# One more unit of the first MLP layer by seven products in four stages, and a pair of transposes moved

## The chip, the cores and the metric

The kernel runs on one core of a Trainium2 chip. The metric is the device time of one execution in microseconds (us), lower is better. The core has TensorE (PE, with its weight loads shown as PEld), VectorE (DVE), ScalarE (ACT), GpSimd (POOL) and SyncE (SP); each works through a queue of its own in order, and DMA transfers are issued from the queues of SP and POOL (and, at the very end, ACT).

## The reference

Attention with a forget gate, followed by a two-layer MLP with tanh-GELU. In the kernel the products are in bf16 with sums in f32.

```python
# q, k, v: (8, 8, 576, 64); f: (8, 8, 576)
scores = q @ k.T / sqrt(64)
cum = cumsum(log(clip(f, 1e-4, 1)))
attn = softmax(where(causal, scores + cum[:, None] - cum[None, :], -1e9))
x = (attn @ v).transpose(0, 2, 1, 3).reshape(4608, 512)
h = x @ w_in                      # 512 x 2048
out = gelu_tanh(h) @ w_out        # 2048 x 512, out is (4608, 512) f32
```

## The kernel before

The attention is done for 16 groups i of four heads (two groups in each of the 8 batches), the MLP for 9 chunks c of 512 rows. A batch has 576 rows and a chunk 512, so the attention runs somewhat ahead. Nothing is scheduled by a planner: a table of words, one for each stage, is the program order, and every engine takes its own instructions from it in that order (`play`). The front table does groups 0 to 6 and chunks 0 and 1; then stage c, for c from 2 to 8, plays `TABLES[c]`: the rest of the second layer of chunk c-1, the first layer of chunk c, and the second layer of chunk c mixed with the attention of groups q2 = 2c+2, q3 = 2c+3 and q4 = 2c+4. Stages 2 to 6 have attention work, 7 and 8 none.

The words that matter here:

- `P.k`: one pair of the first layer, 256 of the 2048 columns of h for the 512 rows: 8 products on PE of 512 columns each (two blocks of 128 columns of h, four input blocks), into a two-bank PSUM tile of pool psS (`P.k.1`: the tile of pool psO, which the attention's outputs use too), then one GELU on ACT (L369, L376).
- `R.k`: a unit by seven products, three words long. It gives the same as the pairs P.k and P.(k+4) in Strassen's manner (Winograd's form): seven blocks of four products with 256 columns (`multiply`, L417) into four half tiles pa, pb (pool psS) and pc, pd (pool psM), with five passes on DVE between them (L432, L423) and four GELUs (L428). The order of the blocks is pa, pb, pc, pd, pa in the first word, pc in the second, pd in the third.
- `T`: four subtractions of blocks of x for the unit of the next chunk, on DVE, 128 x 512 elements each (`x_sums`, L390). They are written over the x of the chunk that is done.
- `K.k.n`: one of the four sums of blocks of w_in that unit k needs (`w_sums`, L405), on DVE. Sums 0 to 2 are written over the x of an old chunk (`HOMES`), sum 3 over a block of w_in itself, after which the plain pairs P.k and P.(k+4) can't be done any more.
- `O`, `F`, `f`: so many steps of the second layer, also by seven products (`seven_products`, L504). O.512 is what is left of the last chunk; its last step ends with an addition on DVE (L529) that frees a bank of pool psM, and a store.
- `G`: sums of the GELU outputs on DVE (L483 to L489). `X` and `Y`: ACT's tables for exp and GELU.
- `S.i.r`: scores of a third of a group on PE and exp on ACT (L256, L264). `M.i.r`: causal masks on POOL (L270). `D`, `V`: denominators and outputs, products on PE, then DVE (L343 to L347, L355). `VW.i`: the values weighted, on POOL (L210). `CL.i`: a copy of a part of them on DVE (L215).
- `TK.i`, `TQ.i`: transposes of k and q on DVE (L193). `LK.i`, `LQ.i`: loads of them, issued by POOL (L187), into buffers that the transposes of two groups before have read. `LV`: loads of v, issued by SP (L164).

Both pools of PSUM that the unit uses have two tiles: psS with tag s (scores, pairs, pa and pb) and psM with tag m (second layer, pc and pd).

Of the kernel before, what the change touches and what calls it, by code (L numbers as in the profile page):

```python
# [16 lines left out]
def kernel(  # L17
# [53 lines left out]
    """  # L71

    FRONT = """
        TQ.0 B.2.256 TK.1 SB TR LP.2@LQ.0 B.2.128 CW S.0.0 B.5.384 B.1.256 Z TQ.1 vw.0.0 S.0.2 WI.0 LQ.2 M.0.0 B.3.384 H.1.0.1
        LP.3 B.1.256 vw.1.0 WI.1@LU.4 W H.1.1.1 WI.3 B.2.256 WI.2 H.1.0.0 M.1.0.1 D.0.0 M.1.0.0 H.0.1.1 V.0.0.0 H.0.1.0 B.2.256 M.0.1 H.1.1.0 V.0.1.0
        D.1.0 H.0.3.0 B.2.128 V.1.0.0 LX.1.1 H.0.3.1 V.1.1.0 m.0.3.2 H.1.3.0 m.0.3.4 B.1.256 VW.1.1 H.1.3.1 B.4.128 vw.0.1 D.0.1 M.1.3 S.1.2 M.1.1 LK.2
        V.0.1.1 V.0.0.1 WO.0 J.0.1 D.1.1 J.0.0 WO.1@LV.1.1 V.1.1.1 V.1.0.1 J.0.3 WO.2@WI.1 VW.3 J.1.0 WO.3 LK.3 LQ.3 J.1.1 TQ.2 J.1.3 LQ.4
        LX.1.0@WO.2 TK.2 J.0.2 J.1.2 X LK.4 F.0.6 TK.3 B.3.256 S.2.0 LK.5 F.0.9 S.2.2 F.0.10 S.2.1 TQ.3 TQ.4 F.0.10 LV.2.0@LK.5 m.2.1 vw.2
        TK.4 S.3.0 f.0.1 M.2.2 CL.2 LQ.5 M.2.0 D.2 f.0.6 S.3.1 m.3.0 F.0.6 V.2.0 S.3.2 TK.5 LK.6 M.3.2 f.0.7 V.2.1 CL.3
        S.4.1 m.3.1 LQ.6 F.0.6 TQ.5 H.4.2.1 D.3 H.4.0.1 LQ.7 VW.4 H.4.0.0 V.3.1 v.3.0 f.0.3 H.4.2.0 CL.4 I.1.0 m.4.1 U.0 LV.2.1@LQ.5 I.1.4  # L80
        TQ.6 m.4.2.3 I.1.1 I.1.5 U.1 LV.3.0@LQ.7 m.4.2.2 TK.6 G.0 M.4.0 I.1.2 I.1.3 U.3 I.1.6 I.1.7 G.1.1.2 U.2 X F.1.14 S.5.0 f.1.28 S.5.1 D.4 M.5.0 f.1.16
# [2 lines left out]
    """

    HOMES = {1: 0, 3: 1}
    TABLES = {}
    TABLES.update(dict.fromkeys((2, 5), """
        Y O.512 P.0 P.1 TK.q3 TQ.q3 LK.q5 LQ.q5 TK.q4 TQ.q4 LK.q6 LQ.q6 LV P.4 P.5 G.0 P.2 P.3 P.6 P.7 G.1.1.2 X F.10 S.q3.0
        D.q2 M.q3.0 f.22 S.q3.1 V.q2.0 M.q3.1 VW.q3 f.18 S.q3.2 V.q2.1 M.q3.2 CL.q3 f.16 S.q4.0 D.q3 M.q4.0 f.18 S.q4.1 V.q3.0  # L90
        M.q4.1 VW.q4 f.9 V.q3.1 f.7 S.q4.2 M.q4.2 CL.q4
    """))
    TABLES.update(dict.fromkeys((3,), """
        Y O.512 P.0 P.1 TK.q3 TQ.q3 LK.q5 LQ.q5 TK.q4 TQ.q4 LK.q6 LQ.q6 LV K.1.0 K.1.1 K.1.2 P.4 P.5 G.0 P.2 P.3 P.6 P.7 G.1.1.2
        X F.10 S.q3.0 D.q2 M.q3.0 f.22 S.q3.1 V.q2.0 M.q3.1 VW.q3 f.18 S.q3.2 V.q2.1 M.q3.2 CL.q3 f.16 S.q4.0 D.q3 M.q4.0 f.18
        S.q4.1 V.q3.0 M.q4.1 VW.q4 f.9 V.q3.1 f.7 S.q4.2 M.q4.2 CL.q4
    """))
    TABLES.update(dict.fromkeys((4,), """
        Y O.512 P.0 P.1 TK.q3 TQ.q3 LK.q5 LQ.q5 TK.q4 TQ.q4 LK.q6 LQ.q6 LV K.3.0 K.3.1 K.3.2 P.4 P.5 G.0 P.2 P.3 P.6 P.7 G.1.1.2
        X F.10 S.q3.0 D.q2 M.q3.0 f.22 S.q3.1 V.q2.0 M.q3.1 VW.q3 f.18 S.q3.2 V.q2.1 M.q3.2 CL.q3 f.16 S.q4.0 D.q3 M.q4.0 f.18  # L100
        S.q4.1 V.q3.0 M.q4.1 VW.q4 f.9 V.q3.1 f.7 S.q4.2 M.q4.2 CL.q4
    """))
    TABLES.update(dict.fromkeys((6,), """
        Y O.512 P.0 P.1 TK.q3 TQ.q3 LK.q5 LQ.q5 LV P.4 P.5 G.0 P.2 P.3 P.6 P.7 G.1.1.2 X F.10 S.q3.0 D.q2 M.q3.0 f.22 S.q3.1
        V.q2.0 M.q3.1 VW.q3 f.18 S.q3.2 V.q2.1 M.q3.2 CL.q3 f.16 D.q3 f.18 V.q3.0 v.q3.1 T K.1.3 K.3.3 f.18
    """))
    TABLES.update(dict.fromkeys((7,), """
        Y O.512 P.0.1 R.1 P.4.1 R.1 R.1 R.3 P.2.1 R.3 G.0.1.2 P.6 R.3 G.0.3.4 G.1.1.2 T
    """))
    TABLES.update(dict.fromkeys((8,), """  # L110
        O.512 P.0.1 R.1 P.4.1 R.1 R.1 R.3 P.2.1 R.3 G.0.1.2 P.6 R.3 G.0.3.4 G.1.1.2
    """))

    singles = ctx.enter_context(tc.tile_pool(name="singles", bufs=1))
    ostage_pool = ctx.enter_context(tc.tile_pool(name="ostage", bufs=3))
# [664 lines left out]
```

## Time and profile before

| | before |
|---|---|
| time, median of 3 runs | 330.25 us (330.21 to 332.17) |
| profiled execution, its span | 328.4 us |
| PE busy | 316.9 us (96%), 5421 products |
| DVE busy | 206.4 us (63%), 323 instructions |
| ACT busy | 201.7 us (61%) |
| POOL busy | 110.6 us (34%) |
| stages 2 to 6 by the starts of their first layers | 34.85, 34.48, 34.48, 34.48, 32.86 us |
| stages 7 and 8 | 25.74 us, 29.09 us to the end |
| first layer of a stage with eight pairs | 13.81 us |
| first layer of stages 7 and 8 (four pairs, two units) | 13.03 and 13.01 us |
| granted TensorE clock | 1.00 throughout |

The profile shows one execution; its span lies 1.85 us below the median of the timed runs. Busy time of PE counts the pipelined products with modelled ends; the steps from start to start in the chain of waits tell the time that a product takes of the stream. Stage starts (first product of P.0) are at 102.42, 137.27, 171.75, 206.23, 240.71, 273.57 and 299.31 us. A group in the timeline names line, engine, operation, output and inputs, shapes and count.

### The profile page before, as it was taken

The page shows a single profiled execution, that of the slowest core. Times are in us where ns is not written, and L with a number is a line of the kernel's source. Part 1 is how long each engine was busy: PE and PEld are TensorE (multiplying, and loading weights), DVE is VectorE, ACT ScalarE, POOL GpSimd, SP SyncE. Part 2 cuts the span into 40 slices and gives each one's busy share as a digit, 9 for nine tenths or more (in the row PEclk, how much of TensorE's full clock was granted, in tenths as well). Part 3 has the DMA queues.
Part 4 walks back from the last instruction along what each step waited for, and adds up shares of the span by engine and source line. Part 5 has one row for each costly group of instructions (what it writes and reads, how often), then busy time and mean ns, then how long its engine had stood idle before and what let it go on. Part 6 is the DMA issues. An engine that isn't in the chain of part 4 may idle for free.

```text
span 328.4 us, 11961 instructions
## 1 busy us (share of the span) xinstructions
PE 316.9 (96%) x5421; PEld 206.5 (63%) x5421; DVE 206.4 (63%) x323; ACT 201.7 (61%) x231; POOL 110.6 (34%) x155
## 2 busy tenths in 40 slices
...
GB/s 123 210 214 215 168 230 199 167 165 24 36 40 94 236 208 31 94 187 108 37 68 182 140 37 36 160 122 36 36 66 0 36 21 81 2 32 98 0 35 96
DMA packets 44323, 33.42 MB, mean 102 GB/s; under 512 B 27488, under 2 KB 37856, under 8 KB 44272
## 3 DMA queue, kind: packets, MB, share of 16 engines
...
q8 instruction: 42, 0.69, 0.9%
...
## 4 chain that ended last, share of the span: by engine, by line
PE 86%; DMA 3%; DVE 3%; ACT 3%; POOL 2%; issue 2%; POOLq 0%; DVEq 0%; ACTq 0%
PE ps_h L369 29%; PE ps_w L504 25%; PE po L324 9%; PE ps_s L256 8%; PE pso L574 4%; PE ps_h L458 4%; DMA v_nat<-in_v_dram 2%; PE ps_cd L417 2%; ACT pt L264 2%; PE ps_ab L417 2%; PE po_m L310 1%; POOL vw L210 1%; DMA out_dram<-o_st 1%; POOL v_nat L164 0%; PE ps_o L324 0%
## 5 line engine op out<-in xcount | busy, mean ns | idle before, releaser
L264 ACT ACTIVATE pt<-ps_s 128x1024 bf16<-128x1024 f32 (+2 forms) x100 | 93.7, 988 | 39.4 <-PE ps_s L256 34.9
L369 PE MATMUL ps_h<-xT,w_in_sb 128*128 128x512 bf16 x448 | 99.0, 379 | 0.0
L376 ACT ACTIVATE gT<-ps_h 128x1024 bf16<-128x1024 f32 x56 | 57.2, 1022 | 49.9 <-PE ps_h L369 48.3
L270 POOL TENSOR_SCALAR_AFFINE_SELECT pt<-pt 128x512 bf16<-128x512 bf16 (+3 forms) x65 | 38.2, 597 | 132.9 <-ACT pt L264 131.8
L369 PEld LDWEIGHTS <-w_in_sb 128*128 128x128 bf16 x448 | 43.8, 98 | 50.1 <-issue 0.4
L504 PEld LDWEIGHTS <-gT 128*32 128x32 bf16 (+1 forms) x1253 | 50.9, 97 | 6.4 <-issue 1.7
L504 PE MATMUL ps_w<-w_out_sb,gT 128*32 128x256 bf16 (+1 forms) x1056 | 46.9, 273 | 0.0
L504 PEld LDWEIGHTS <-gsum 128*32 128x32 bf16 (+1 forms) x1256 | 38.9, 97 | 2.7 <-issue 1.4
L256 PE MATMUL ps_s<-qT,kT 32*128 32x64 bf16 (+5 forms) x896 | 36.8, 263 | 0.3 <-ACT pt L264 0.2
L483 DVE TENSOR_TENSOR gsum<-gT 128x1024 bf16<-128x1024 bf16 x16 | 11.0, 689 | 35.2 <-ACT gT L376 35.2
L504 PE MATMUL ps_w<-usum,gsum 128*32 128x256 bf16 (+1 forms) x832 | 30.7, 273 | 1.0 <-ACT snap L525 0.7
L355 DVE TENSOR_TENSOR xT<-po,rb 128x576 bf16<-128x576 f32 x26 | 19.6, 755 | 18.9 <-PE po L324 18.6
L193 DVE STREAM_TRANSPOSE kT<-k_c 128x576 f32<-128x576 f32 x16 | 20.0, 1247 | 17.8 <-DMA k_c<-in_k_dram 17.8
L210 POOL TENSOR_TENSOR vw<-v_nat,wT 128x1280 bf16<-128x1280 f32 (+1 forms) x13 | 30.4, 2338 | 0.1
L529 DVE TENSOR_TENSOR o_st<-ps_w,snap 128x512 f32<-128x512 f32 x31 | 21.3, 689 | 13.2 <-PE ps_w L504 11.8
L256 PEld LDWEIGHTS <-kT 32*128 32x128 bf16 x896 | 16.9, 93 | 17.4 <-issue 12.6
L324 PE MATMUL po<-pt,vw 128*32 128x64 bf16 (+4 forms) x624 | 22.5, 279 | 0.0
L324 PEld LDWEIGHTS <-vw 128*32 128x32 bf16 x672 | 14.3, 96 | 10.6 <-issue 3.7
L193 DVE STREAM_TRANSPOSE qT<-q_c 128x576 f32<-128x576 f32 x16 | 19.9, 1242 | 1.1 <-PE ps_s L256 0.5
L164 POOL DMA_DIRECT2D v_nat<-in_v_dram x20 | 15.3, 776 | 4.6 <-DMA w_out_sb<-in_moe_w_out_dram 4.6
L504 PE MATMUL ps_w<-usum,gT 128*128 128x256 bf16 (+1 forms) x197 | 16.4, 273 | 0.0
L574 PE MATMUL pso<-w_out_sb,gT 128*32 128x512 bf16 (+1 forms) x115 | 15.6, 380 | 0.0
...
## 6 DMA issues: line engine op xcount, KB each, us to landing
...
```

The source lines that it names most:

```text
L193: nc.vector.transpose(out=dst.rearrange("p s c -> p (s c)").bitcast(FP32) .rearrange("p (t a) -> p a t", a=S // 32), in_=src.rearrange("p ...
L210: eng.tensor_mul(vw[i % 2][:, t0:t1], vb[:, t0:t1, h0:h0 + 4, :], wT[:, i, t0:t1, :].unsqueeze(3).to_broadcast([128, t1 - t0, 4, D]))
L256: nc.tensor.matmul(tiles[h // 2][:, h % 2, c0:c0 + nq], key_columns(i, key, h, c), qq[32 * h:32 * h + 32, q0:q0 + nq, c], start=(c == 0 an ...
L264: nc.scalar.activation(p[:, 2 * g:2 * g + 2, off:off + n], t[:, :, 0:n], AF.Exp, scale=scale)
L270: nc.gpsimd.affine_select(out=x, in_=x, compare_op=ALU.is_ge, fill=0.0, base=0, pattern=pattern, channel_multiplier=-1)
L324: nc.tensor.matmul(po[r0:r0 + w.shape[-1], 448 + q0:448 + q0 + nq], w, p[:, h, col:col + nq], start=(key in (0, "low")), stop=(key in ("lo ...
L355: nc.vector.tensor_mul(xT[:, 2 * u + x, S * b + s0:S * b + s1], po, rbs[i, part])
L369: nc.tensor.matmul(ph[:, j, :], w_in_sb[:, dt, 128 * ft:128 * ft + 128], xT[:, dt, CH * c:CH * (c + 1)], start=(dt == 0), stop=(dt == N_DT ...
L376: nc.scalar.activation(gT[:, 2 * pr:2 * pr + 2, :], ph, AF.Gelu_apprx_tanh)
L504: nc.tensor.matmul(ps[c0:c0 + width, n, cols[0]:cols[1]], x[:, j, 128 * n + c0:128 * n + c0 + width], w[:, j, cols[0]:cols[1]], start=(fir ...
L529: nc.vector.tensor_add(st, ps, kept[name])
L574: nc.tensor.matmul(pso[c0:c0 + cols, :], gT[:, ft, 128 * n + c0:128 * n + c0 + cols], w_out_sb[:, ft, :], start=(ft == 0), stop=(ft == N_F ...
```

## The change

Unit 1 is done by seven products in stages 3 to 6 too, where before it was done so only in stages 7 and 8; so P.1 and P.5 go there, P.0 and P.4 use the tile of pool psO, and T stands at the end of stages 2 to 5 (at the end of stage 6 it stood before). The weight sums of unit 1 (K.1), which stood in the first layer of stage 3 and at the end of stage 6, move into stage 2. Those of unit 3 (K.3.0 to K.3.2) move from the first layer of stage 4 to places behind V steps of the same stage. In stages 3 to 5 TK.q4 and TQ.q4 move from before the rest of the first layer to behind V.q2.0, and LK.q6 and LQ.q6 to behind M.q3.2; TK.q3, TQ.q3, LK.q5, LQ.q5 and LV now follow the unit. The front table has the same words in other line breaks. Line numbers below L112 grow by 4.

The tables of stage 2 to 6, before and after (the parts that stay the same within a table are left out):

```diff
 # stage 2
-  ... S.q3.1 V.q2.0 M.q3.1 VW.q3 f.18 S.q3.2 V.q2.1 M.q3.2 CL.q3 ... S.q4.1 V.q3.0
-  M.q4.1 VW.q4 f.9 V.q3.1 f.7 S.q4.2 M.q4.2 CL.q4
+  ... S.q3.1 V.q2.0 K.1.0 M.q3.1 VW.q3 f.18 S.q3.2 V.q2.1 K.1.1 M.q3.2 CL.q3 ... S.q4.1 V.q3.0 K.1.2
+  M.q4.1 VW.q4 f.9 V.q3.1 f.7 S.q4.2 M.q4.2 CL.q4 K.1.3 T
 # stages 3 and 5 (K.1.0 K.1.1 K.1.2 in stage 3 alone)
-  Y O.512 P.0 P.1 TK.q3 TQ.q3 LK.q5 LQ.q5 TK.q4 TQ.q4 LK.q6 LQ.q6 LV K.1.0 K.1.1 K.1.2 P.4 P.5 G.0 P.2 P.3 P.6 P.7 G.1.1.2
-  X F.10 S.q3.0 D.q2 M.q3.0 f.22 S.q3.1 V.q2.0 M.q3.1 VW.q3 f.18 S.q3.2 V.q2.1 M.q3.2 CL.q3 f.16 S.q4.0 D.q3 M.q4.0 f.18
-  S.q4.1 V.q3.0 M.q4.1 VW.q4 f.9 V.q3.1 f.7 S.q4.2 M.q4.2 CL.q4
+  Y O.512 P.0.1 R.1 P.4.1 R.1 R.1 TK.q3 TQ.q3 LK.q5 LQ.q5 LV P.2 G.0 P.3 P.6 P.7 G.1.1.2 X F.10 S.q3.0 D.q2 M.q3.0 f.22 S.q3.1 V.q2.0 TK.q4 TQ.q4
+  M.q3.1 VW.q3 f.18 S.q3.2 V.q2.1 M.q3.2 LK.q6 LQ.q6 CL.q3 f.16 S.q4.0 D.q3 M.q4.0 f.18 S.q4.1 V.q3.0 M.q4.1 VW.q4 f.9 V.q3.1 f.7 S.q4.2 M.q4.2
+  CL.q4 T
 # stage 4: as stages 3 and 5, and
-  ... LV K.3.0 K.3.1 K.3.2 P.4 P.5 ...
+  ... V.q2.1 K.3.0 M.q3.2 ... V.q3.0 K.3.1 M.q4.1 VW.q4 f.9 V.q3.1 K.3.2 f.7 S.q4.2 M.q4.2 CL.q4 T
 # stage 6
-  Y O.512 P.0 P.1 TK.q3 TQ.q3 LK.q5 LQ.q5 LV P.4 P.5 G.0 P.2 P.3 P.6 P.7 G.1.1.2 X F.10 ...
-  ... f.16 D.q3 f.18 V.q3.0 v.q3.1 T K.1.3 K.3.3 f.18
+  Y O.512 P.0.1 R.1 P.4.1 R.1 R.1 TK.q3 TQ.q3 LK.q5 LQ.q5 LV P.2 G.0 P.3 P.6 P.7 G.1.1.2 X F.10 ...
+  ... f.16 D.q3 f.18 V.q3.0 v.q3.1 T K.3.3 f.18
```

Stages 7 and 8 keep their tables (two units each, 1 and 3). Over the whole program PE gets 4 x 28 products of 256 columns for 4 x 16 of 512, DVE 4 x 9 more passes (five in a unit, four in T), and ACT four GELUs of half size for two in each of the four stages.

More of the change, by code (lines that the diff above doesn't have):

```diff
@@ L73 @@
     FRONT = """
[L74 to L81, printed above, removed]
@@ L82 @@
-        S.5.2 V.4.0 m.5.2.3 f.1.10 VW.5 V.4.1 CL.5 m.5.2.2 LQ.8 S.6.0 f.1.10 M.5.1 D.5 f.1.7 S.6.1 V.5.1 f.1.12 V.5.0 vw.6 S.6.2
-        m.6.1 M.6.2.2 m.6.0 m.6.2.3 LK.7 LK.8 CL.6 LX.3.1@LK.6
+        TQ.0 B.2.256 TK.1 SB TR LP.2@LQ.0 B.2.128 CW S.0.0 B.5.384 B.1.256 Z TQ.1 vw.0.0 S.0.2 WI.0 LQ.2 M.0.0 B.3.384 H.1.0.1 LP.3 B.1.256 vw.1.0
+        WI.1@LU.4 W H.1.1.1 WI.3 B.2.256 WI.2 H.1.0.0 M.1.0.1 D.0.0 M.1.0.0 H.0.1.1 V.0.0.0 H.0.1.0 B.2.256 M.0.1 H.1.1.0 V.0.1.0 D.1.0 H.0.3.0 B.2.128
+        V.1.0.0 LX.1.1 H.0.3.1 V.1.1.0 m.0.3.2 H.1.3.0 m.0.3.4 B.1.256 VW.1.1 H.1.3.1 B.4.128 vw.0.1 D.0.1 M.1.3 S.1.2 M.1.1 LK.2 V.0.1.1 V.0.0.1 WO.0
@@ new lines @@
+        J.0.1 D.1.1 J.0.0 WO.1@LV.1.1 V.1.1.1 V.1.0.1 J.0.3 WO.2@WI.1 VW.3 J.1.0 WO.3 LK.3 LQ.3 J.1.1 TQ.2 J.1.3 LQ.4 LX.1.0@WO.2 TK.2 J.0.2 J.1.2 X
+        LK.4 F.0.6 TK.3 B.3.256 S.2.0 LK.5 F.0.9 S.2.2 F.0.10 S.2.1 TQ.3 TQ.4 F.0.10 LV.2.0@LK.5 m.2.1 vw.2 TK.4 S.3.0 f.0.1 M.2.2 CL.2 LQ.5 M.2.0 D.2
+        f.0.6 S.3.1 m.3.0 F.0.6 V.2.0 S.3.2 TK.5 LK.6 M.3.2 f.0.7 V.2.1 CL.3 S.4.1 m.3.1 LQ.6 F.0.6 TQ.5 H.4.2.1 D.3 H.4.0.1 LQ.7 VW.4 H.4.0.0 V.3.1
+        v.3.0 f.0.3 H.4.2.0 CL.4 I.1.0 m.4.1 U.0 LV.2.1@LQ.5 I.1.4 TQ.6 m.4.2.3 I.1.1 I.1.5 U.1 LV.3.0@LQ.7 m.4.2.2 TK.6 G.0 M.4.0 I.1.2 I.1.3 U.3
@@ L84 @@
+        I.1.6 I.1.7 G.1.1.2 U.2 X F.1.14 S.5.0 f.1.28 S.5.1 D.4 M.5.0 f.1.16 S.5.2 V.4.0 m.5.2.3 f.1.10 VW.5 V.4.1 CL.5 m.5.2.2 LQ.8 S.6.0 f.1.10 M.5.1
+        D.5 f.1.7 S.6.1 V.5.1 f.1.12 V.5.0 vw.6 S.6.2 m.6.1 M.6.2.2 m.6.0 m.6.2.3 LK.7 LK.8 CL.6 LX.3.1@LK.6
     """
@@ L87 @@
     TABLES = {}
-    TABLES.update(dict.fromkeys((2, 5), """
-        Y O.512 P.0 P.1 TK.q3 TQ.q3 LK.q5 LQ.q5 TK.q4 TQ.q4 LK.q6 LQ.q6 LV P.4 P.5 G.0 P.2 P.3 P.6 P.7 G.1.1.2 X F.10 S.q3.0
-        D.q2 M.q3.0 f.22 S.q3.1 V.q2.0 M.q3.1 VW.q3 f.18 S.q3.2 V.q2.1 M.q3.2 CL.q3 f.16 S.q4.0 D.q3 M.q4.0 f.18 S.q4.1 V.q3.0
-        M.q4.1 VW.q4 f.9 V.q3.1 f.7 S.q4.2 M.q4.2 CL.q4
-    """))
-    TABLES.update(dict.fromkeys((3,), """
-        Y O.512 P.0 P.1 TK.q3 TQ.q3 LK.q5 LQ.q5 TK.q4 TQ.q4 LK.q6 LQ.q6 LV K.1.0 K.1.1 K.1.2 P.4 P.5 G.0 P.2 P.3 P.6 P.7 G.1.1.2
-        X F.10 S.q3.0 D.q2 M.q3.0 f.22 S.q3.1 V.q2.0 M.q3.1 VW.q3 f.18 S.q3.2 V.q2.1 M.q3.2 CL.q3 f.16 S.q4.0 D.q3 M.q4.0 f.18
-        S.q4.1 V.q3.0 M.q4.1 VW.q4 f.9 V.q3.1 f.7 S.q4.2 M.q4.2 CL.q4
@@ L97 @@
[L97 to L105, printed above, removed]
@@ L106 @@
-    """))
-    TABLES.update(dict.fromkeys((7,), """
+    TABLES[2] = """
+        Y O.512 P.0 P.1 TK.q3 TQ.q3 LK.q5 LQ.q5 TK.q4 TQ.q4 LK.q6 LQ.q6 LV P.4 P.5 G.0 P.2 P.3 P.6 P.7 G.1.1.2 X F.10 S.q3.0 D.q2 M.q3.0 f.22 S.q3.1
+        V.q2.0 K.1.0 M.q3.1 VW.q3 f.18 S.q3.2 V.q2.1 K.1.1 M.q3.2 CL.q3 f.16 S.q4.0 D.q3 M.q4.0 f.18 S.q4.1 V.q3.0 K.1.2 M.q4.1 VW.q4 f.9 V.q3.1 f.7
+        S.q4.2 M.q4.2 CL.q4 K.1.3 T
+    """
+    TABLES[3] = """
+        Y O.512 P.0.1 R.1 P.4.1 R.1 R.1 TK.q3 TQ.q3 LK.q5 LQ.q5 LV P.2 G.0 P.3 P.6 P.7 G.1.1.2 X F.10 S.q3.0 D.q2 M.q3.0 f.22 S.q3.1 V.q2.0 TK.q4 TQ.q4
+        M.q3.1 VW.q3 f.18 S.q3.2 V.q2.1 M.q3.2 LK.q6 LQ.q6 CL.q3 f.16 S.q4.0 D.q3 M.q4.0 f.18 S.q4.1 V.q3.0 M.q4.1 VW.q4 f.9 V.q3.1 f.7 S.q4.2 M.q4.2
+        CL.q4 T
@@ new lines @@
+    """
+    TABLES[4] = """
+        Y O.512 P.0.1 R.1 P.4.1 R.1 R.1 TK.q3 TQ.q3 LK.q5 LQ.q5 LV P.2 G.0 P.3 P.6 P.7 G.1.1.2 X F.10 S.q3.0 D.q2 M.q3.0 f.22 S.q3.1 V.q2.0 TK.q4 TQ.q4
+        M.q3.1 VW.q3 f.18 S.q3.2 V.q2.1 K.3.0 M.q3.2 LK.q6 LQ.q6 CL.q3 f.16 S.q4.0 D.q3 M.q4.0 f.18 S.q4.1 V.q3.0 K.3.1 M.q4.1 VW.q4 f.9 V.q3.1 K.3.2
+        f.7 S.q4.2 M.q4.2 CL.q4 T
+    """
+    TABLES[5] = """
+        Y O.512 P.0.1 R.1 P.4.1 R.1 R.1 TK.q3 TQ.q3 LK.q5 LQ.q5 LV P.2 G.0 P.3 P.6 P.7 G.1.1.2 X F.10 S.q3.0 D.q2 M.q3.0 f.22 S.q3.1 V.q2.0 TK.q4 TQ.q4
+        M.q3.1 VW.q3 f.18 S.q3.2 V.q2.1 M.q3.2 LK.q6 LQ.q6 CL.q3 f.16 S.q4.0 D.q3 M.q4.0 f.18 S.q4.1 V.q3.0 M.q4.1 VW.q4 f.9 V.q3.1 f.7 S.q4.2 M.q4.2
+        CL.q4 T
```

7 lines of the change are left out of this document (6 added, 1 removed).

## The prediction

> **What bounds the kernel now.** I read the busy shares first, then the chain of waits, then the busy time by stage, and last the timelines of VectorE (DVE) and GpSimd (POOL) around one boundary between stages.
>
> ```profile
> PE 316.9 (96%) x5421; PEld 206.5 (63%) x5421; DVE 206.4 (63%) x323; ACT 201.7 (61%) x231; POOL 110.6 (34%) x155
> ```
>
> PE is busy for 96% of the span; nothing else passes 63%. In the waits of PE from 90 us on there are two, of 0.3 us each. So an edit gains only the PE time that it removes, and loses whatever it makes PE wait. What a first layer (the pairs P and the seven-product units R) costs is read in two stretches: stage 4, eight plain pairs, and stage 7, four pairs and two units.
>
> ```profile
> 171.75:185.56 13.81, 13.81 (x67) 6.32 (x65) 8.96 (x13) 9.15 (x10) 3.41 (x6) 1.00 0.96 194
> 273.57:286.60 13.03, 13.03 (x90) 8.66 (x89) 9.81 (x15) 7.27 (x11) 0.00 (x0) 1.00 0.13 42
> ```
>
> Columns: stretch, length, then busy time (count) of PE, PEld, DVE, ACT, POOL, then clock, DMA share, GB/s. PE is full in both, the clock is 1.00, and two units shorten the layer by 0.78 us. The chain of waits gives the steps of a unit:
>
> ```profile
> 273.57 1.73 PE ps_h L369 x8
> 275.29 0.87 PE ps_ab L417 x8
> 276.17 0.87 PE ps_cd L417 x8
> 277.04 0.44 PE ps_ab L417 x4
> ```
>
> Start, length, work. A pair P is 1.73 us; a block of four products is 0.44 us. From the start of P.0 the second block (pb, the first to read T's sums) comes at +2.17, the fourth (pd) at +3.04, the fifth (pa again) at +3.48.
>
> **Removed and added on PE.** A unit is 28 products of 256 columns, 0.109 us each (0.87 / 8): 3.06 us. It replaces P.1 and P.5, 2 x 1.73 = 3.45 us. Gain 0.39 us, four times: **-1.57 us**, the 0.78 / 2 of the stretches.
>
> The Trainium skill (TensorE: Matmul & The Clock Gate, section Back-to-back issue gap) has a rule against this: sustained, 512 columns take about 131 ns and 128 columns 81 ns, so half-wide products cost far more than half. By it a unit, estimated at 98 ns for 256 columns, would be 28 x 98 = 2.74 us against 16 x 131 = 2.10, so four units would add 2.6 us and the total below would be 335.8 us. The rows (216 ns and 109 ns, gapless) do not agree, and follow the same section's N/2.4 + 2.5 instead; I give this less than 0.01.
>
> **Transposes and loads that move.** TK.q4 and TQ.q4 take 2 x 1.08 us of DVE (their starts in the timeline are 1.09 us apart). Behind V.q2.0 they run, in stage 3's times, from 159.1 to 161.2; the next DVE step, V.q2.1's multiplication, starts at 161.3 instead of 160.83 and frees the PSUM bank at 162.0; D.q3's product asks for it at 163.15. Cost 0, with 1.1 us to spare. The pt masks of POOL beside these transposes take 0.64 us as elsewhere. LK.q6 and LQ.q6 (0.53 to 0.59 us of POOL each) go behind M.q3.2, into POOL's gap from 163.3 to 165.3, and are used 30 us later against 5.8 and 7.3 us to land: 0. LK.q5 and LQ.q5 go 8 us later, used 25 us after that: 0. On SP nothing changes places; the loads of v go out about 3 us later and are read 30 us after: 0.
>
> **The unit's own chain on DVE** is five passes of 0.69 us, 0.8 us apart when dependent; in stages 7 and 8 PE does not wait inside it. Here the room is the 2.17 us that the transposes left. G.0 follows about 10.4 to 13.2 us after the stage's start, and its sums are first read by item 32 of the second layer, at +18.5: 0 while it is under 5 us late. On ACT, P.4.1 needs P.0's bank: that gelu would end at 174.9 (table loaded to 173.9, plus 1.0) and P.4.1 asks at 171.75 + 1.73 + 2.18 = 175.66: 0.
>
> **K and T on DVE: where I see the loss.** T is four subtractions of 0.41 us and now stands at the end of stages 2 to 5, behind CL.q4 and ahead of the last addition (L529) of O.512, whose bank pd needs. Stage 4's start, DVE then POOL:
>
> ```profile
> 169.06 0.76 DVE L355 TENSOR_TENSOR xT<-po,rb 128x576 bf16<-128x576 f32 x1 [0.97 <-PE po L324]
> 169.73 0.68 DVE L529 TENSOR_TENSOR o_st<-ps_w,snap 128x512 f32<-128x512 f32 x1
> 171.61 0.22 DVE L215 COPY vw<-vw 64x256 bf16<-64x256 bf16 x1 [1.20 <-POOL vw L210]
> 171.86 0.69 DVE L529 TENSOR_TENSOR o_st<-ps_w,snap 128x512 f32<-128x512 f32 x1
> ...
> 169.25 2.33 POOL L210 TENSOR_TENSOR vw<-v_nat,wT 128x1280 bf16<-128x1280 f32 x1
> 172.44 1.23 POOL L270 TENSOR_SCALAR_AFFINE_SELECT pt<-pt 128x512 bf16<-128x512 bf16 x2 [0.86 <-ACT pt L264]
> ```
>
> CL (L215) waits for POOL's VW until 171.61. T starts at 171.86, alone it ends at 173.5, the addition at 174.2, and pd asks at 171.75 + 3.04 = 174.79: no wait. But two masks (L270) start at 172.44, in the middle of T, and elsewhere in this trace DVE and POOL exclude each other:
>
> ```profile
> 86.47 0.68 DVE L487 TENSOR_TENSOR gT<-gT 128x1024 bf16<-128x1024 bf16 x1
> 87.06 2.82 DVE L489 TENSOR_TENSOR gsum<-gT,gsum 128x1024 bf16<-128x1024 bf16 x1
> ...
> 86.64 2.71 POOL L210 TENSOR_TENSOR vw<-v_nat,wT 128x1280 bf16<-128x1280 f32 x1
> ...
> 102.24 1.53 DVE L299 TENSOR_TENSOR pt<-pt,causal 128x512 bf16<-128x512 bf16 x3
> ...
> 102.77 0.72 POOL L270 TENSOR_SCALAR_AFFINE_SELECT pt<-pt 128x512 bf16<-128x512 bf16 x1 [12.22 <-ACT pt L264]
> ```
>
> L489 takes 0.69 us elsewhere and 2.82 here: it ends 0.55 us after VW does. VW took 2.71 instead of 2.33: it began when L487 was done, ahead of L489. With the mask at 102.77 the third L299 took 0.86 us instead of 0.42. These are DVE passes with both inputs in SBUF, as T and K are; additions from PSUM (L529, L355) beside the same POOL work keep their 0.69 and 0.76.
>
> Taking turns, the boundary goes: T1, T2 to 172.69; mask to 173.2; T3; mask; T4. With full durations T4 ends at 174.6 and the addition at 175.3: pd waits 0.5, and the fifth block 0.15 more for the copy p1 behind that addition: 0.65. With the hand-over 0.14 us before an end, as VW's 0.38 us delay shows it, 0.35. I take **0.5** for the boundaries 3/4 and 5/6. At 2/3 K.1.3 stands ahead of T, 0.41 us later: 0.55 to 1.0, I take **0.75**. At 4/5 K.3.2 stands behind V.q3.1, at 204.21, inside VW (203.73 to 206.06): it ends at 206.4, CL at 207.3, and T begins behind the first mask (206.92); T2 then ends at 208.9 where pb asks at 206.23 + 2.17 = 208.40, and pd and the fifth block wait again: 0.9 to 1.3, I take **1.15**. The other K steps fall ahead of masks (K.1.0 at 123.83 before 123.96, K.1.2 at 133.5 before 134.10) or displace one by 0.4 us, hidden on both sides: 0. Stage 6's T already stands there, with POOL idle: 0.
>
> **The sum.** -1.57 + 0.75 + 0.5 + 1.15 + 0.5 = **+1.3 us**: a profiled span of 328.4 + 1.3 = 329.7, and on the median of 330.25 (1.85 us more than the span, kept) **331.6 us**. Under 1%, which is about what a measurement of this kernel can tell from no change.
>
> **Rivals.** *No exclusion for T* (A): T and the masks run side by side and every boundary wait is 0: 330.25 - 1.57 = 328.7. For it: T has never stood beside POOL work, and only two events show the exclusion. Against: L299 is of T's size and type and was held by the same kind of mask. The Trainium skill (SBUF: State Buffer, section SBUF: two separate sides) says that such a pass and a GpSimd instruction lock the shared ports for the whole instruction, which would exclude A; the two rows agree with it.
>
> *The masks win every turn* (B), the slower side: at each boundary T1 comes to the port after the first mask and POOL keeps it through both. T then runs from 173.7 to 175.1, the addition to 175.7: pd waits 0.9 and the fifth block 0.2, 1.1 at 3/4 and 5/6, 1.5 at 2/3 and 4/5, 5.2 in all: 330.25 - 1.57 + 5.2 = 333.9. It decides as soon as CL ends over 0.58 us later than now (171.86 against 172.44) and the two masks, 0.6 us apart, let nothing between. For it: POOL issues them back to back, and K.3.2 does push CL so at one boundary. Against: L487 let VW in between two DVE passes, and at three boundaries nothing delays VW.
>
> **How the numbers follow.** Forecast 0.66, A 0.19, B 0.10, others 0.05 (0.02 of them a gain over 1%, the rest split). Faster by over 1%: 0.02. Slower: B and a tail of the forecast, 0.12. Same: 0.86. The range reaches below A's 328.7 by the scatter of a run and up to 333.2, between the forecast's upper bounds (3.4 us of waits, 332.1) and B; that leaves B's half and the tails out.
>
> **What would show it.** In the profile after: first layers of stages 3 to 6 with 28 products of 0.109 us (else the gain fails); T (L390, new line 394) with single passes of 0.7 us or more beside masks, K.3.2 of about 2.2 us, POOL's masks up to 0.8 us; PE waiting before the fourth block of the unit for the addition, 0.2 to 0.5 us, and most at the start of stage 5. T at 0.42 us each and no wait of PE there means A. Stages 3 to 5 of 34.1 us each mean A as well, 34.6 to 35.2 the forecast. A wait of PE in mid-stage, for the bank that V.q2.1 frees, would prove the moved transposes mis-costed.

## The result, and the profile after

The changed kernel takes 333.29 us in the median of 19 runs, against 330.55 us for the kernel before in as many beside it: a ratio of 1.0075, 95% interval 1.0053 to 1.0097. So it is slower by some 2.5 us by the ratio (2.7 by the medians), which is under 1%. The forecast was 331.6 us; the measured median lies 1.7 us above it, just past the 333.2 us named as the end of the range, while the ratio lies inside it (333.2 over the forecast's own 330.25 is 1.0089). Ratios, and the spans of runs below, leave out the few executions that were over 1.5% longer than the fastest of their kernel. The profiled execution has a span of 330.7 us against 328.4, at the same clock. Over the runs of the changed kernel the median span is 331.6 us, so 0.9 us of a typical run is not in this profile (0.2 us in the kernel before, 328.65 for 328.4).

The busy line of the page after:

```profile
PE 316.1 (96%) x5449; PEld 211.4 (64%) x5469; DVE 231.4 (70%) x363; ACT 202.1 (61%) x239; POOL 111.7 (34%) x155
```

Next the busy time by stage, from start to start of the first layers (stretch, length, then busy time and count of PE, PEld, DVE, ACT, POOL, then clock, DMA share, GB/s). These are stages 3 to 6 of the kernel after, and the first layer of stage 4 alone:

```profile
137.60:173.07 35.47, 34.49 (x715) 23.34 (x715) 26.81 (x43) 23.70 (x29) 12.86 (x16) 1.00 0.49 99
173.07:207.26 34.19, 34.08 (x714) 23.31 (x714) 26.63 (x39) 23.79 (x29) 12.94 (x16) 1.00 0.51 100
207.26:242.62 35.36, 34.47 (x715) 23.23 (x715) 26.74 (x41) 23.60 (x29) 11.60 (x14) 1.00 0.40 85
242.62:275.54 32.92, 32.42 (x665) 22.62 (x665) 25.30 (x42) 20.15 (x25) 6.79 (x8) 1.00 0.10 32
```

```profile
173.07:186.49 13.42, 13.31 (x77) 7.42 (x77) 10.56 (x16) 9.41 (x12) 2.54 (x4) 1.00 0.81 151
```

Before, stages 3 to 5 took 34.48 us each and stage 6 took 32.86. Stage 4 is now shorter by 0.3, and its first layer by 0.39 (13.81 to 13.42): the gain is there. Stages 3 and 5 are longer by 0.99 and 0.88, stage 6 by 0.06. Together with 0.14 in stage 2, 0.35 ahead of it (where the program has the same words) and 0.09 behind stage 6, this is the 2.2 us by which the span grew.

The waits of PE from 90 us on say what fills stages 3 and 5. Columns: who waited, for whom, total, times, longest:

```profile
PE ps_cd L421 <- DVE o_st L533: 0.7, 2, 0.3
PE po L328 <- issue: 0.6, 1, 0.6
PE ps_ab L421 <- DVE xT L394: 0.4, 1, 0.4
PE ps_w L508 <- DVE o_st L533: 0.3, 1, 0.3
PE po L328 <- POOL pt L274: 0.3, 1, 0.3
```

The last two were there before (as L504 and L324). New are the two that the prediction named (the unit waits for the late addition L533, and for T, L394), and one that it did not have: PE stands still among V's products (L328), and "issue" says that it waits for nothing that the profile shows.

The start of stage 5 in the timelines of VectorE and GpSimd:

```profile
205.31 2.12 DVE L409 TENSOR_TENSOR xT<-w_in_sb,xT 128x512 bf16<-128x512 bf16 x1
207.35 0.68 DVE L533 TENSOR_TENSOR o_st<-ps_w,snap 128x512 f32<-128x512 f32 x1
208.06 0.67 DVE L219 COPY vw<-vw 64x256 bf16<-64x256 bf16 x1
208.74 2.02 DVE L394 TENSOR_TENSOR xT<-xT 128x512 bf16<-128x512 bf16 x4
210.69 0.68 DVE L533 TENSOR_TENSOR o_st<-ps_w,snap 128x512 f32<-128x512 f32 x1
...
204.82 2.33 POOL L214 TENSOR_TENSOR vw<-v_nat,wT 128x1280 bf16<-128x1280 f32 x1
208.01 1.22 POOL L274 TENSOR_SCALAR_AFFINE_SELECT pt<-pt 128x512 bf16<-128x512 bf16 x2 [0.87 <-ACT pt L268]
```

K.3.2 (L409) takes 2.12 us inside VW, as the prediction drew it; CL (L219) takes 0.67 us for 0.22 beside the first mask (L274), and T starts at 208.74. The chain of waits goes through this place:

```profile
208.74 0.79 DVE xT L394
209.53 0.02 issue
209.55 0.43 DVE xT L394
...
210.77 0.61 DVE o_st L533
211.38 0.04 issue
211.42 0.60 PE ps_cd L421 x4
212.02 0.60 PE ps_ab L421 x4
```

T's first pass takes 0.79 us beside the second mask, the next 0.43 alone. Blocks pb, pd and the second pa start 0.60, 0.51 and 0.17 us late: 1.28 us. In the same way PE waits 0.64 us at the start of stage 3 and 0.47 at that of stage 6. At the start of stage 4 it waits 0:

```profile
172.57 1.68 DVE L394 TENSOR_TENSOR xT<-xT 128x512 bf16<-128x512 bf16 x4
...
173.91 1.42 POOL L274 TENSOR_SCALAR_AFFINE_SELECT pt<-pt 128x512 bf16<-128x512 bf16 x2 [1.61 <-ACT pt L268]
```

The masks start 1.34 us after T here, where the prediction had 0.58. The cause is the new stall shortly before: it delays the scores, and with them the masks, but not CL (in the run noload below, without the stall, the wait is there).

The stall itself, PE first, then the loads on POOL:

```profile
168.87 0.84 PE L328 MATMUL po<-pt,vw 128*32 128x512 bf16 x21
170.27 0.21 PE L328 MATMUL po<-pt,vw 128*32 128x64 bf16 x3 [0.56 <-issue]
...
163.99 0.59 POOL L191 DMA_DIRECT2D k_c<-in_k_dram  x1
164.58 0.54 POOL L191 DMA_DIRECT2D q_c<-in_q_dram  x1
```

The 24 products of V are of one step; PE stops between the 21st and the 22nd, and the profile names no releaser. What is different from before, beside the moved transposes, is the two loads LK.q6 and LQ.q6 that now run while PE does this. The trace also records packets of 16 KB on an "instruction" queue: 42 in the execution, and PE has 5449 products and 5469 weight loads, some 260 for each packet. The trace does not name the engine that they are for; by this count, and because they come closer together where the products are short, they are taken for PE's instructions here. In the second layer of stage 3 they come every 3.4 to 4.2 us before (161.76, 165.94, 169.29). After, they come at 162.56 and then 167.79, 5.2 us apart, and PE goes on 2.5 us after the start of the late one. So the theory for the experiments was: the loads beside the second layer delay PE's instructions. The rivals were the moved transposes as the cause of that stall, DVE's longer work (and not the masks beside it) as the cause of the waits at the boundaries, and units that cost more than the sum says.

### The profile page after: what moved, and what is told of

The parts are those of the page before. It is cut to its first block, busy times and chain, and to the rows that moved or that the text cites. A ratio compares the mean times of both kernels' runs of the same rounds, so it can differ in the third digit from the quotient of the medians.

```text
span 330.7 us, 12089 instructions
## 1 busy us (share of the span) xinstructions
PE 316.1 (96%) x5449; PEld 211.4 (64%) x5469; DVE 231.4 (70%) x363; ACT 202.1 (61%) x239; POOL 111.7 (34%) x155
## 4 chain that ended last, share of the span: by engine, by line
PE 82%; DVE 6%; POOL 5%; issue 3%; ACT 3%; DMA 1%; POOLq 0%; DVEq 0%; ACTq 0%
PE ps_h L373 23%; PE ps_w L508 23%; PE ps_s L260 9%; PE po L328 8%; PE ps_h L462 4%; PE pso L578 4%; PE ps_cd L421 4%; PE ps_ab L421 3%; ACT pt L268 2%; POOL vw L214 2%; DVE xT L394 2%; PE po_m L314 1%; PE idle_ps L239 1%; DVE o_st L533 1%; POOL v_nat L168 1%
## 5 line engine op out<-in xcount | busy, mean ns | idle before, releaser
L373 PE MATMUL ps_h<-xT,w_in_sb 128*128 128x512 bf16 x368 | 85.5, 379 | 0.8
L274 POOL TENSOR_SCALAR_AFFINE_SELECT pt<-pt 128x512 bf16<-128x512 bf16 (+3 forms) x65 | 39.1, 611 | 115.2 <-ACT pt L268 114.2
L380 ACT ACTIVATE gT<-ps_h 128x1024 bf16<-128x1024 f32 x48 | 49.0, 1022 | 44.2 <-PE ps_h L373 43.9
L373 PEld LDWEIGHTS <-w_in_sb 128*128 128x128 bf16 x384 | 37.5, 98 | 40.9 <-issue 0.4
L508 PE MATMUL ps_w<-w_out_sb,gT 128*32 128x256 bf16 (+1 forms) x1056 | 47.1, 273 | 0.0
L533 DVE TENSOR_TENSOR o_st<-ps_w,snap 128x512 f32<-128x512 f32 x31 | 21.2, 687 | 12.5 <-PE ps_w L508 11.1
L427 DVE TENSOR_TENSOR h_st<-ps_cd,h_st 128x512 f32<-128x512 f32 x32 | 21.6, 689 | 7.0 <-PE ps_cd L421 5.1
L328 PE MATMUL po<-pt,vw 128*32 128x64 bf16 (+4 forms) x624 | 22.7, 279 | 0.6 <-issue 0.6
L328 PEld LDWEIGHTS <-vw 128*32 128x32 bf16 x672 | 14.4, 96 | 11.4 <-issue 4.4
L191 POOL DMA_DIRECT2D k_c<-in_k_dram x16 | 9.2, 575 | 30.0 <-DVE kT L197 24.4
```

Source lines behind the costliest of these rows:

```text
L274: nc.gpsimd.affine_select(out=x, in_=x, compare_op=ALU.is_ge, fill=0.0, base=0, pattern=pattern, channel_multiplier=-1)
L328: nc.tensor.matmul(po[r0:r0 + w.shape[-1], 448 + q0:448 + q0 + nq], w, p[:, h, col:col + nq], start=(key in (0, "low")), stop=(key in ("lo ...
L373: nc.tensor.matmul(ph[:, j, :], w_in_sb[:, dt, 128 * ft:128 * ft + 128], xT[:, dt, CH * c:CH * (c + 1)], start=(dt == 0), stop=(dt == N_DT ...
L380: nc.scalar.activation(gT[:, 2 * pr:2 * pr + 2, :], ph, AF.Gelu_apprx_tanh)
L427: nc.vector.tensor_add(st, ps, y)
L508: nc.tensor.matmul(ps[c0:c0 + width, n, cols[0]:cols[1]], x[:, j, 128 * n + c0:128 * n + c0 + width], w[:, j, cols[0]:cols[1]], start=(fir ...
```

## The experiments

All were run beside the kernel before. First the measurements in one place. "Boundary" is the sum of PE's waits in the units at the starts of stages 3, 4, 5, 6, "stall" the longest stop of PE inside stage 3 or 4, both in the profiled execution and worked out from the starts of the products (PE's own waits in the views count up to 0.2 us less).

| kernel | ratio to before (95%) | median us | boundary us | stall us |
|---|---|---|---|---|
| changed | 1.0075 (1.0053 to 1.0097) | 333.29 | 0.64, 0, 1.28, 0.47 | 0.73 |
| nomask | 1.0013 (0.9982 to 1.0044) | 331.41 | 0, 0, 0.14, 0 | 0.47 |
| no_t | 1.0002 (0.9970 to 1.0034) | 330.94 | 0, 0, 0, 0 | 2.18 |
| noload | 1.0047 (1.0019 to 1.0074) | 332.16 | 0.65, 0.47, 1.39, 0.46 | 0 |
| moved_only | 1.0032 (1.0004 to 1.0060) | 332.18 | no units there | 1.72 |
| loads_only | 1.0047 (1.0026 to 1.0068) | 332.29 | no units there | 1.44 |
| trans_only | 1.0000 (0.9981 to 1.0018) | 330.59 | no units there | not read |
| e_back | 1.0075 (1.0053 to 1.0097) | 333.46 | 0.64, 0.46, 1.38, 0.46 | 0 |
| early | 1.0079 (1.0065 to 1.0092) | 333.19 | 0.65, 0.47, 1.38, 0.46 | 1.19, another wait |
| k32 | 1.0040 (1.0013 to 1.0067) | 331.80 | 0.65, 0, 0.16, 0.46 | 0.70 |
| split_t | 1.0012 (0.9990 to 1.0033) | 330.84 | 0, 0, 0, 0 | 0.43 |
| split_t_early | 0.9976 (0.9960 to 0.9993) | 329.54 | 0, 0, 0, 0 | 0 |
| split_back | 0.9969 (0.9947 to 0.9990) | 329.59 | 0, 0, 0, 0 | 0 |

### The waits at the boundaries

**nomask**

```diff
 # stages 2 to 5
-  S.q4.2 M.q4.2 CL.q4 ... T
+  S.q4.2 CL.q4 ... T
```

> The changed kernel with M.q4.2, the two masks of POOL at the end of stages 2 to 5, left out (so a part of the causal mask is missing). Theory of the ports (T's subtractions and POOL's masks exclude each other): T takes 1.6 us at the ends of stages 2, 3 and 5, PE's waits of 0.64 us at the start of stage 3 and 0.47 us at the start of stage 6 are gone, that of 1.28 us at the start of stage 5 falls to 0.3 to 0.6 us, because K.3.2 still stands inside VW; ratio to the kernel before 0.996 to 0.999. Rival, T's mere length ahead of the addition: the waits stay as they are, ratio 1.0075.

With the masks gone T takes its own time, although K.3.2 is as late as before:

```profile
204.10 2.12 DVE L407 TENSOR_TENSOR xT<-w_in_sb,xT 128x512 bf16<-128x512 bf16 x1
206.15 0.68 DVE L531 TENSOR_TENSOR o_st<-ps_w,snap 128x512 f32<-128x512 f32 x1
206.85 0.22 DVE L217 COPY vw<-vw 64x256 bf16<-64x256 bf16 x1
207.09 1.68 DVE L392 TENSOR_TENSOR xT<-xT 128x512 bf16<-128x512 bf16 x4
```

1.68 us against 2.02, CL 0.22 against 0.67, and T starts 0.44 us sooner after K.3.2 does (2.99 for 3.43). Only 0.14 us is left of the waits. At the starts of stages 3 and 6, where nothing else changes, 0.64 and 0.47 us go to 0 with the same DVE work, so these waits come from POOL's masks beside DVE's passes, and not from the length of DVE's work. (At the start of stage 5 a stall of 0.47 us just before, in stage 4, hides a part of the wait.) The ratio of 1.0013 is above the expected 0.996 to 0.999: that stall is a part of the difference, the rest is not located.

**no_t**

```diff
 # stages 2 to 5
-  ... CL.q4 T
+  ... CL.q4
```

> The changed kernel without T at the end of stages 2 to 5 (the units of stages 3 to 6 then work on old sums). Both theories, ports and length: no wait of PE at the four starts of stages, so that the gain of 1.57 us shows, ratio 0.995 to 0.997. If the ratio stays above 1.000, something that is not T costs the rest: the stall of 0.73 us in mid-stage 3 of the profile after, or the like.

No wait is left at any boundary, stage 6 takes 32.46 us against 32.92, and stage 5 34.08 against 35.36. But stage 3 takes 36.28 us: the stall is there, and it is larger than in the changed kernel.

```profile
170.56 0.21 PE L328 MATMUL po<-pt,vw 128*32 128x64 bf16 x3 [2.02 <-issue]
```

It stands at the same products of V, with the instruction packets at 161.49 and 168.29, 6.8 us apart. T has no part in it, and without T the kernel is still no faster than before.

### The stall in mid-stage

**noload**

```diff
 # stages 3 and 4
-  M.q3.2 LK.q6 LQ.q6 CL.q3
+  M.q3.2 CL.q3
```

> The changed kernel with LK.q6 and LQ.q6, the two moved loads, left out in stages 3 and 4 (so those groups use old k and q). Theory of the fetch: the stall of 0.73 us in mid-stage 3, in which PE waits for nothing that the trace shows, comes from PE's instruction packet (16 KB) taking 1.4 us beside these loads; without them it is gone, runs scatter less, and the ratio falls to about 1.004, the forecast of 1.3 us. Rival, the stall has nothing to do with the loads: ratio 1.0075 and a stall of that kind somewhere in stages 3 to 5.

The stall is gone from stages 3 and 4, and the packets are 3.4 to 4.0 us apart again where the loads had been. (This profile has a stop of 0.8 us in stage 2, of which more below.) The DMA view of five us in stage 3, first the changed kernel (163 to 168), then this one (163.3 to 168.3):

```profile
q0 software_dynamic: 201, 0.43, 55.4%
q8 instruction: 1, 0.02, 1.7%
```

```profile
DMA packets 2, 0.03 MB, mean 7 GB/s; under 512 B 0, under 2 KB 0, under 8 KB 0
q8 instruction: 2, 0.03, 2.7%
```

The columns are packets, MB and the share of the 16 engines: with the loads on q0 one instruction packet comes in these five us, without them two, and they are all that the DMA engines move then. With no stall ahead of it, the wait at the start of stage 4 is back too (0.47), and the four boundaries are 2.97 us together, where the prediction had 2.9. The ratio fell from 1.0075 to 1.0047, to about the expected 1.004, but the two intervals overlap.

**moved_only**

```diff
 # the kernel before, stages 3 to 5
-  P.1 TK.q3 TQ.q3 LK.q5 LQ.q5 TK.q4 TQ.q4 LK.q6 LQ.q6 LV ... V.q2.0 M.q3.1 ... M.q3.2 CL.q3
+  P.1 TK.q3 TQ.q3 LK.q5 LQ.q5 LV ... V.q2.0 TK.q4 TQ.q4 M.q3.1 ... M.q3.2 LK.q6 LQ.q6 CL.q3
```

> The kernel before with the second part alone: TK.q4 and TQ.q4 behind V.q2.0, LK.q6 and LQ.q6 behind M.q3.2 in stages 3 to 5, no unit added. The prediction's step: 0, ratio 0.999 to 1.001, no new wait of PE. Theory of the fetch: stalls of 0.5 to 0.7 us of PE in mid-stage 3 or 4, 3 to 5 us after the loads are issued, and a ratio of 1.001 to 1.004.

The second part of the change alone costs about 1 us, without any unit: stage 3 goes from 34.48 to 36.30 us, with one stop of 1.72 us at 171.52 and packets 6.1 us apart (162.97, 169.10). The other stages keep 34.48. Two kernels take this part in two:

**loads_only**

```diff
 # the kernel before, stages 3 to 5
-  TK.q4 TQ.q4 LK.q6 LQ.q6 LV ... M.q3.2 CL.q3
+  TK.q4 TQ.q4 LV ... M.q3.2 LK.q6 LQ.q6 CL.q3
```

> The kernel before, with one edit: in stages 3 to 5 the loads LK.q6 and LQ.q6 stand behind M.q3.2 (as in the changed kernel), while the transposes TK.q4 and TQ.q4 stay in the first layer. Theory (the loads beside the second layer delay PE's instruction packets): PE stalls 0.5 to 2.2 us in stage 3 between 165 and 173 us, with two packets over 5 us apart there, stages 3 to 5 otherwise 34.48; ratio 1.002 to 1.006. Rival (the moved transposes on DVE are what costs): no stall, stages 34.48 each, ratio 1.000 within 0.002.

**trans_only**

```diff
 # the kernel before, stages 3 to 5 (LK.q4 LQ.q4 in 4 and 5 alone)
-  TK.q3 TQ.q3 LK.q5 LQ.q5 TK.q4 TQ.q4 LK.q6 LQ.q6 LV ... V.q2.0 M.q3.1
+  LK.q4 LQ.q4 TK.q3 TQ.q3 LK.q5 LQ.q5 LV ... V.q2.0 TK.q4 TQ.q4 M.q3.1
```

> The kernel before, with the other half: in stages 3 to 5 TK.q4 and TQ.q4 stand behind V.q2.0 (as in the changed kernel); the loads stay out of the second layer, and go out as LK.q4 and LQ.q4 in the first layers of stages 4 and 5, ahead of TK.q3. Theory (loads beside the second layer): no stall of PE in stages 3 to 5, which stay at 34.4 to 34.6; ratio 1.000 within 0.002. Rival (transposes): a wait of PE of 0.5 us or more behind V.q2.1 or D.q3 in each of stages 3 to 5; ratio 1.003 to 1.006.

The loads alone give 1.0047, the transposes alone 1.0000, and their intervals do not overlap. (Of trans_only only the timed runs are read.) In loads_only the waits of PE and the stop itself:

```profile
PE ps_w L509 <- issue: 1.3, 1, 1.3
PE ps_w L509 <- DVE o_st L534: 0.3, 1, 0.3
PE po L329 <- POOL pt L275: 0.3, 1, 0.3
```

```profile
170.87 0.29 PE L509 MATMUL ps_w<-w_out_sb,gsum 128*32 128x256 bf16 x3 [1.28 <-issue]
...
163.55 0.59 POOL L192 DMA_DIRECT2D k_c<-in_k_dram  x1
164.14 0.54 POOL L192 DMA_DIRECT2D q_c<-in_q_dram  x1
```

This time PE stops among products of the second layer, not of V, again with two packets 6.4 us apart (162.05, 168.47). So the place isn't bound to a step of the program. The two loads beside the second layer of stages 3 and 4 are enough to cost 1.5 us; the transposes are free. This is the pair that settles which half of the move costs.

### Putting the loads elsewhere

**e_back**

```diff
 # the changed kernel, stages 3 to 5
-  ... TK.q3 TQ.q3 LK.q5 LQ.q5 LV P.2 ... V.q2.0 TK.q4 TQ.q4 M.q3.1 ... M.q3.2 LK.q6 LQ.q6 CL.q3
+  ... TK.q3 TQ.q3 LK.q5 LQ.q5 TK.q4 TQ.q4 LK.q6 LQ.q6 LV P.2 ... V.q2.0 M.q3.1 ... M.q3.2 CL.q3
```

> The changed kernel with the second part undone: TK.q4, TQ.q4, LK.q6 and LQ.q6 stand again in the first layer of stages 3 to 5, now behind the unit; the four units, T and K are as changed. Theory (gain of 1.57 us, waits for T at the starts of stages 3 to 6, and about 1 us for the loads): no stall in mid-stage of stages 3 and 4, boundary waits 0.6, 0.5, 1.2 and 0.5 (the second no longer hidden behind a stall), so 1.3 us over before: ratio 1.003 to 1.005, and under 1.0075 of the changed kernel. Rival (the loads cost nothing on the median; the units themselves cost more than the sum says): 1.007 to 1.009. If DVE, which gets two more transposes ahead of G.0, comes late with the sums of the gelu outputs, PE waits near 18 us into the stage: 1.01 or more.

A miss: the profile looks as the theory says (no stall, waits of 2.94 us, a span of 329.9, 1.4 more than before), but the time is that of the changed kernel. The profiled execution is among the shortest: the spans of the runs go from 329.7 to 331.7 us, median 330.8. And what lies outside the span, 1.65 to 1.78 us in every run of before, is 1.7 to 3.7 here, median 2.3. The profile shows one packet of instructions at 331.5 us, behind the end of the span. The kernels whose profiles have such a packet (noload, no_t and split_t too) had 2.1 to 2.6 us outside the span in that execution, and those without one 1.9 or less. That accounts for some 0.6 us; the 0.9 us by which the median span exceeds the profiled one was not seen in any profile and stays open, as in the changed kernel. So this run does not show that the loads cost the changed kernel anything on the median.

**early**

```diff
 # the changed kernel
 # stages 4 and 5
-  ... R.1 TK.q3 TQ.q3 LK.q5 LQ.q5 LV P.2 ...
+  ... R.1 LK.q4 LQ.q4 TK.q3 TQ.q3 LK.q5 LQ.q5 LV P.2 ...
 # stages 3 to 5
-  M.q3.2 LK.q6 LQ.q6 CL.q3
+  M.q3.2 CL.q3
```

> The changed kernel with the two moved loads put elsewhere, the whole output kept: instead of LK.q6 and LQ.q6 in the middle of stages 3 and 4, LK.q4 and LQ.q4 in the first layer of stages 4 and 5, ahead of TK.q3. Theory of the fetch (PE's instruction packets come late beside loads that run while PE works through its short products): no stall in the middle of stages 3 and 4, instruction packets there 3.5 to 4.5 us apart; the waits at the starts of stages stay (about 0.6, 0.5, 1.3 and 0.5 us); ratio 1.003 to 1.005. Rival, the stalls have another cause: they stay, ratio 1.0075.

A miss as well. The stall in mid-stage went, but another wait of 1.19 us came in the first layer of stage 4:

```profile
181.34 0.69 DVE L427 TENSOR_TENSOR h_st<-ps_cd,h_st 128x512 f32<-128x512 f32 x1 [1.86 <-DMA out_dram<-o_st]
```

```profile
PE ps_h L373 <- ACT gT L380: 1.0, 1, 1.0
```

The unit's last pass on DVE waits 1.86 us for a store of the output to land, ACT's GELU comes late, and PE waits for its bank. The loads are issued at 174.42 and 175.01, ahead of that store. There is no stop of PE for instructions here, but something else is late behind the loads: this store takes 5.9 us to land, where it takes 2.3 us in the changed kernel and in e_back. That it is late for their sake is argued from these times only.

### What beats both kernels

**k32**

```diff
 # the changed kernel, stage 4
-  V.q3.0 K.3.1 M.q4.1 VW.q4 f.9 V.q3.1 K.3.2 f.7
+  V.q3.0 K.3.1 K.3.2 M.q4.1 VW.q4 f.9 V.q3.1 f.7
```

> The changed kernel with K.3.2 right behind K.3.1, before the mask and VW.q4 of POOL, instead of behind V.q3.1. Theory of the ports: K.3.2 takes 0.42 us instead of 2.12, CL and T of stage 4 come 0.7 us earlier, and PE's wait at the start of stage 5 falls from 1.28 to about 0.5 us; ratio 0.002 lower than the changed kernel's 1.0075. Theory of mere length: DVE has as much to do as before, no change at that boundary.

K.3.2 (L408) and T (L393) in the timeline of VectorE:

```profile
203.25 0.42 DVE L408 TENSOR_TENSOR xT<-w_in_sb,xT 128x512 bf16<-128x512 bf16 x1
206.74 2.42 DVE L393 TENSOR_TENSOR xT<-xT 128x512 bf16<-128x512 bf16 x4
```

K.3.2 takes 0.42 us here, ahead of VW, and T starts 0.5 us ahead of the masks (207.23), where in the changed kernel it starts 0.7 us behind the first of them. One sum out of VW's time takes the wait at the start of stage 5 from 1.28 to 0.16 us. (Part of this belongs to a stall of 0.40 us just before, which delays PE and the masks.) The stall in stage 3 stays, 0.70 us.

**split_t**

```diff
 # stages 2 to 5: T's first subtraction in mid-stage, K.1.3 and K.3.1 behind the f.18 that follows, K.3.2 behind V.q3.0
-  f.16 S.q4.0 D.q3 M.q4.0 f.18 ... CL.q4 T
+  f.16 T.0 S.q4.0 D.q3 M.q4.0 f.18 ... CL.q4
 # stages 3 to 6: the other three ("N") in the first layer, behind the late addition
-  Y O.512 P.0.1 R.1 P.4.1 R.1 R.1
+  Y O.512 N.1.3 P.0.1 R.1 N.2 P.4.1 R.1 R.1
```

> The changed kernel with T taken apart: its first subtraction behind f.16 in mid-stage where POOL rests, the second and fourth behind the last addition of O.512 instead of ahead of it, the third behind the first word of the unit; K.1.3, K.3.1 and K.3.2 moved to places where POOL rests. The loads stay where the change put them. Theory of the ports: no wait of PE at the starts of stages 3 to 6 (gain of 1.57 us shows there: stages 4 and 5 take 34.1 us); theory of the fetch: stalls of 0.5 to 2.2 us in mid-stage 3 or 4 stay; ratio 0.997 to 1.002.

**split_t_early** is split_t with the loads as in early; **split_back** is split_t with transposes and loads as in e_back.

> The two together: T taken apart as in the run split_t, loads early as in the run early. Both theories: neither waits at the starts of stages nor stalls in mid-stage; what is left is the change of 28 products of 256 columns for 16 of 512, four times: 1.57 us less than the kernel before, ratio 0.994 to 0.997. If it stays above 0.999, a third cost is hidden in the change.

> The version with T taken apart (T.0 behind f.16, the other three subtractions in the first layer, K.1.3 and K.3.1 behind f.18, K.3.2 behind V.q3.0), with the transposes TK.q4, TQ.q4 and the loads LK.q6, LQ.q6 of stages 3 to 5 back in the first layer, behind the unit. Theory: no wait at any boundary and no stall in stages 3 to 5, 34.08 us each; stage 2 at 35.2 as in the two versions with T apart; ratio 0.995 to 0.998, like the version with early loads. Rival (the first layer has no room on DVE for T's three, the unit's five passes and four transposes): G.0 late, PE waits near 18 us into the stage, ratio over 1.000.

With T apart no boundary waits: the late addition (L529) is no longer behind T, and of the two passes of T that follow it pb needs the first and pd the second. From split_back, at the start of stage 5:

```profile
206.35 0.69 DVE L529 TENSOR_TENSOR o_st<-ps_w,snap 128x512 f32<-128x512 f32 x1
206.96 1.66 DVE L390 TENSOR_TENSOR xT<-xT 128x512 bf16<-128x512 bf16 x2
208.54 0.68 DVE L432 COPY snap<-ps_ab 128x512 f32<-128x512 f32 x1
```

Two passes of T still take 0.85 and 0.89 us beside the masks, but both end ahead of the blocks that read them: pb starts at 208.25, pd at 209.12, without a gap. The waits of PE from 100 us on are those of before:

```profile
PE ps_w L504 <- DVE o_st L529: 0.3, 1, 0.3
PE po L324 <- POOL pt L270: 0.3, 1, 0.3
PE ps_s L256 <- issue: 0.2, 1, 0.2
```

Stages 3 to 5 take 34.07 to 34.09 us and stage 6 32.45, 0.4 less each than before: the whole gain of the units. split_t_early missed its expected 0.994 to 0.997 narrowly; in its profile stage 2 is 0.4 us longer than before (35.25 against 34.85), and the stretch ahead of it 0.2. Both versions are faster than before, by 0.2 to 0.3%. split_t_early differs from split_t (1.0012) in the place of the loads LK.q6 and LQ.q6 alone, split_back in that of the transposes too. They are 1.2 and 1.4 us faster by the ratios, though their intervals reach that of split_t: with no wait at the boundaries, this is about what the loads cost a kernel with the units in it.

## Why the prediction was right or wrong

- **The gain, -1.57 us: right.** Where nothing waits, stages 3 to 6 are 0.4 us shorter each (34.08 for 34.48; 32.45 for 32.86).
- **The exclusion, and where its price falls: right.** T passes of up to 0.85 us beside masks against 0.42 alone, K.3.2 at 2.12 us, the masks in pairs of 1.22 to 1.55 us for 1.23, and the most at the start of stage 5 are all there. The waits were put at 0.75, 0.5, 1.15 and 0.5 us. Without the loads in the way (noload) they are 0.65, 0.47, 1.39 and 0.46. Rival A (no exclusion) falls by nomask. Rival B (1.1 to 1.5 us at every boundary) falls by the rows: only stage 5's start comes near it. Two sums of this part were too low: the upper bounds of the waits add up to 3.6 us and not 3.4 (332.3 us for 332.1), and Rival B's T, from 173.7 to 175.1, leaves 1.4 us for four subtractions of 0.41 us (with 1.64 it would be about 334.9 us for 333.9). Neither changes the forecast. The Trainium skill (SBUF: State Buffer, section SBUF: two separate sides) has the pair of ports locked for a whole instruction; the 2.12 us of K.3.2, which ends 0.3 us after VW does, agree.
- **The moved transposes, 0: right** (trans_only, 1.0000).
- **The loads LK.q6 and LQ.q6 behind M.q3.2, 0: wrong.** The step looked at the POOL queue that issues them and at the landing time, and both were as it said. It didn't ask what else uses the DMA engines in that stretch. On their own the loads cost 1.5 us (0.0047 of 330.4; interval 0.9 to 2.2 us), beside T taken apart 1.2 to 1.4 us, and leaving them out of the changed kernel saves about 1 us (1.0075 to 1.0047, with intervals that overlap). Of the 1.7 us by which the forecast was short, 0.3 is the median of before, 330.55 in these runs for 330.25. That the loads are the larger part of the rest is likely but not shown, since e_back, without them, is no faster than the changed kernel.
- **The sum, +1.3 us: near, in part by luck.** In the profile after, the gain, the waits at the boundaries (2.39 us together, for the predicted 2.9) and the stall (0.73) come to 1.55 us. The stall that the prediction did not have took the place of the wait at the start of stage 4 that it did have; without the loads (noload) the waits alone are 2.97 us.
- **The wait in mid-stage that "would prove the moved transposes mis-costed"** named one suspect for such a wait. It came, but from the other half of the same move. The sign to tell them by was in the waits: a bank that V.q2.1 frees would have been put down to DVE, and this one is put down to "issue".
- **1.85 us around the span, kept: right for the changed kernel** (median 1.7), but not for all that were built from it (2.3 in e_back).

What stays open is why an instruction packet comes late beside loads (the packets themselves take 0.9 to 1.4 us in either case), why stage 3 suffers more than stage 4, and the 0.9 us by which the median spans of the changed kernel and of e_back exceed their profiles. Most profiles also have a stop of 0.1 to 0.8 us near 125 us, in stage 2 (before too, 0.25). It fits the theory, for transfers fill the DMA engines there as well (in the kernel before, from 118 to 123 us, q1 56.2% and q0 47.1%) and the packet comes 4.3 to 5.65 us after the one before it; but no run changed it.

The loads as the cause are shown by loads_only against trans_only, and borne out by noload and by split_t against the two versions with the loads elsewhere. That the late packet is the link rests on times alone: the ten stops of this kind in stages 3 and 4 of seven profiles all follow a packet that came 5.2 to 6.8 us after the one before it, and PE goes on 2.3 to 2.5 us after its start, whatever the product. The reverse does not hold: in stage 4 of the changed kernel a packet came 5.75 us after the one before it (204.40), and PE did not stop.
